# Causal attention and a channel mix on one core: the eight PSUM banks in one pool, batch 0 in two column ranges, and another order of the start

## The chip, the core and the metric

The kernel runs on one core of one Trainium2 chip. The metric is the device time of one execution in microseconds. The core has a matrix engine (TensorE, PE in the profile), which writes its products to PSUM, a memory of eight banks of 128 x 512 fp32; VectorE (DVE), ScalarE (ACT) and GpSimd (POOL), which work on tiles of 128 partitions in SBUF (DVE and ACT read PSUM too); SyncE (SP), which here only issues transfers; and 16 DMA engines, which serve the transfers issued from SP, ACT and POOL. Every engine runs its own list of instructions in order and waits for the others by semaphores.

## What is computed

Block-causal attention of eight batches, and over its output a channel mix (RWKV style):

```python
# q, k, v: (8 batches, 8 heads, 576, 64); blocks of 64 positions
scores = q @ k.T / sqrt(64)            # only where block(row) >= block(column)
attn   = softmax(scores) @ v
x      = attn as (8, 576, 512)
x_prev = x shifted by one position
xk = mu_k * x + (1 - mu_k) * x_prev    # and xr with mu_r
k  = relu(xk @ w_k)                    # 512 -> 1024
out = sigmoid(xr @ w_r) * (k * k @ w_v)
```

## The kernel before

Each batch goes through these steps, and each step is a *task* that the code adds to a list (`plan.add`), with the engine that it runs on, the tiles that it uses and the tasks that it needs.

* `qkld`: four loads per batch, half of q's or k's heads each (0.59 MB in fp32). Batch 0's come from SP as two transfers each and are cast to bf16 by `qkc` (L229). Those of batches 1 to 7 are casting transfers issued from POOL (L274). `turn` (L292) transposes 32 x 32 blocks on DVE.
* `vld` (L314), `vc` (L229, L223): v in two halves, two transfers each from SP, and a cast to fp16.
* `sc` (L396): scores, in *units* of up to 512 columns of all heads. A unit takes two pairs of banks, half of the heads in each. For batches 0 and 1 the two halves are tasks of their own. `ex` (L417): two exponentials per unit on ACT, which write tile `e`.
* For batches 1 to 7, `av` (L480 for the sums, L491 for the products with v), then the sums' reciprocals (L436, L441, L450 on DVE) and `norm` (L520, L528). For batch 0, the 576 positions are done in three thirds: `sum` (L554), `av` (L568), `norm` (L582).
* The mix: `d` (the difference to the position before, L608, L604) and `mul` (L624, L628), by 128 channels.
* The channel mix by groups `c` of 512 rows: `pk` (L661: eight products with the K weights), `relu` (L674, L676), `sq` (L683, L685), `pr` and `tanh` (L700, L709), `pv` (L730: products with the V weights), `o` (L738) and `store`. Group 0's `pk` is done for 192, 192 and 128 rows.
* `wld`, `wc`: the weights K, R, V are loaded from SP (L252) as fp32 and cast on DVE, ACT or POOL. `mus` loads mu_k and mu_r from SP (L760), `mu1` makes four small tiles of them on DVE.

Nothing decides at run time. `ORDER` is a list of task numbers, in which the instructions are written; each engine gets its own in that order. `PLACE` gives the engine of each task that may go to several. Tiles are in rings (`RINGS`): a task that needs a tile gets, among those that no later-listed task still uses, the one that has been free longest. PSUM has three rings: `s` (two pairs of banks, for scores), `av` (one pair, for the attention products) and `mm` (two single banks, for everything else).

In `ORDER`, a number may have "+n": n products of an identity matrix that nobody reads, ahead of the task (`unread`, L235). In the kernel before no number has it.

At the start, the order on the engines is: SP: batch 0's `qkld`, the first `vld`, two K weights, `mus`, the second `vld`, the other K weights, then v of batches 2 and 1 among the V weights, the R weights last. POOL: four `qkld` of batch 1 and one of batch 2, then a `qkc` of batch 0, more loads, casts. PE: scores of batch 0 with some of batch 1 among them, sums, batch 0's products with v, the rest of batch 1's scores, `pk 0 6`.

Of the kernel before, what the change touches and what calls it, by code (L numbers as in the profile page):

```python
# [66 lines left out]
    "DDPDAPDPAPAPAADAPDPPADPPPPDPPPPDAAAPAAPDPPADDPDPDPPPADADDPPPDAAPDDAPAD"  # L67
    "AADPDAAPADAADADPDDDPAPDAAADAAPDAAAAPAPDPAPDPAAAADPAAAPDDDAAPDPDPAPAPAP"
    "DPAAAADAAPAAAPDDAADDDAAPAAADAPAPDPDAAPDPAADPAAAAAPAPDPAPADAPADAAAAAPDA"
    "DAAAADADDDADAAAPAPAPAPADAAAAADDDAPDP")  # L70


class Plan:
# [17 lines left out]
    def buf(self, ring):  # L91
        return {"ring": ring, "left": 0, "slot": None}

    def issue(self, t):


        for b in t["uses"]:
            if b["slot"] is None:
                ring = self.slots[b["ring"]]
                at = min((s[0], n) for n, s in enumerate(ring) if s[1])[1]  # L100
                ring[at][1] = False
                b["slot"] = at
        t["fn"](t["eng"], t)
        self.issued += 1
        for b in t["uses"]:
            b["left"] -= 1
            if not b["left"]:
                self.slots[b["ring"]][b["slot"]] = [1000 + self.issued, True]
# [18 lines left out]
def kernel(  # L127
# [31 lines left out]
    RINGS = {"ld": 6, "nb": 5, "qkt": 2, "vo": 2, "e": 9, "xt": 1, "tt": 1,  # L159
             "rc": 2, "rt": 1, "d": 2, "xk": 2, "xr": 2, "kr": 4, "k2": 2,  # L160
             "t": 4, "o": 3, "s": 2, "av": 1, "mm": 2}
    plan = Plan(RINGS)
    pools = {}
    for n in RINGS:
        if n in ("xk", "xr"):
            continue
        kw = {"space": PSUM} if n in ("s", "av", "mm") else {}
        pools[n] = ctx.enter_context(
            tc.tile_pool(name="p_" + n, bufs=1, **kw))
# [5 lines left out]
        "ld": ([P, LW], FP), "nb": ([P, LW], BF),  # L175
# [5 lines left out]
        "s": ([P, 2, 512], FP), "av": ([P, 2, 512], FP), "mm": ([P, CH], FP)}  # L181
# [3 lines left out]
             for at in range(n)}  # L185

    def new(buf):

        return slots[buf["ring"], buf["slot"]]
# [43 lines left out]
    spare = {}  # L233

    def unread(t, dst):  # L235

        for _ in range(t["fill"]):
            nc.tensor.matmul(  # L240
                spare.get("at", dst), identb,
                identb[:, :].unsqueeze(1).to_broadcast([P, 4, P]),
                start=True, stop=True)

    def load(key, jobs, nbytes):
        ld = plan.buf("ld")

        def fn(eng, me):  # L250
            for dst, src in jobs(new(ld)):
                nc.sync.dma_start(dst, src)  # L252
        return ld, add(key, ("SP",), fn, uses=[ld], kind="ld",
                       kb=nbytes / 1024, starts=1 if key[4] in "kr" else 2)
# [7 lines left out]
    def add_qk(b, g, n):  # L262
# [4 lines left out]
        ld, nb = plan.buf("ld"), plan.buf("nb")  # L267
# [4 lines left out]
        if b in DIRECT:  # L272
# [3 lines left out]
                    uses=[nb], kind="ldc", kb=P * LW * 4 / 1024)  # L276
        else:
            def fetch(eng, me):
                if b not in HALVES:
                    nc.sync.dma_start(new(ld), rows(GH * g, GH))  # L280
                    return
                for y in range(2):
                    nc.sync.dma_start(new(ld)[y * D:y * D + D],  # L283
                                      rows(GH * y + 2 * g, 2))
            t = add(f"qkld {b} {g} {n}", ("SP",), fetch, uses=[ld], kind="ld",
# [18 lines left out]
    def add_v(b, m):  # L304
# [3 lines left out]
        ld = plan.buf("ld")  # L308
# [24 lines left out]
    def add_w(name, i):  # L333
        if name == "k":
            srcs = [by_quarter(moe_w_k)[i // 2, i % 2]]
        elif name == "r":
            srcs = [moe_w_r.rearrange("(g p f) j -> g p (f j)", g=2, f=2)[i]]
        else:
            srcs = [moe_w_v[(2 * i + h) * P:(2 * i + h + 1) * P]
                    for h in range(2)]  # L340
        w = 2 * CH // len(srcs)
        ld, t = load(f"wld {name} {i}", lambda d: [
            (d[:, h * w:h * w + w], s) for h, s in enumerate(srcs)],
            P * 2 * CH * 4)

        def fn(eng, me):
            s = new(ld)[:, 0:2 * CH]
            if name == "k":
                convert(eng, WK[:, i], s)
            else:  # L350
                dst = (WR if name == "r" else WV)[:, 2 * i:2 * i + 2]
                convert(eng, dst, s.rearrange("p (h j) -> p h j", h=2),
                        0.5 if name == "v" else None)
# [480 lines left out]
```

## Time and profile before

| | |
|---|---|
| median of three runs | 286.56 us (286.09 to 289.16) |
| profiled execution | 286.35 us, of which 284.6 us from the first to the last instruction |
| PE busy | 247.6 us (87%), 4232 matmuls |
| DVE, ACT, POOL busy | 197.6, 175.3, 84.1 us (69%, 62%, 30%) |
| mean granted clock of PE | 0.934 |
| HBM read, written | 33.56 MB, 9.44 MB |

In the profile's rows an instruction has its engine, the line of the kernel, what it writes <- what it reads and the shapes. "x48" is the number of instructions that a row holds. Timeline rows begin with the start and the time from the first to the last of them; what ended the idle time before stands in square brackets, and "issue" means that nothing in the profile shows a wait. Group rows give the busy time and the mean of one in ns. Rows of the chain that ended last begin with start and length, and name engine, tile and line. SPq is SP's queue.

### The profile page before, as it was taken

Reading aid. Unit: us, or ns where it says so; the run is one execution under the profiler, and the core shown is the slowest. Engines: PE = TensorE matmul, PEld = TensorE weight load, DVE = VectorE, ACT = ScalarE, POOL = GpSimd, SP = SyncE. Lnnn points to the kernel's source line nnn. Section 1 sums busy time; section 2 is a strip of 40 time slices with the busy share of each in tenths; the row PEclk is TensorE's granted clock in tenths of the full one; section 3 lists DMA queues with packets and bytes.
Section 4 is the critical chain, followed back from the end, with each engine's and each line's share of the span. In section 5 each row is a group of like instructions: output and inputs, shape, how many; then the busy total and the mean of one; then the engine's idle time right before and its main releaser. Section 6 shows DMA issues by size and latency. Waiting matters only on the chain.

```text
span 284.6 us, 9493 instructions
## 1 busy us (share of the span) xinstructions
PE 247.6 (87%) x4232; PEld 136.8 (48%) x4232; DVE 197.6 (69%) x288; ACT 175.3 (62%) x252; POOL 84.1 (30%) x105
## 2 busy tenths in 40 slices
PE   0056865795889999999999999999999999999995
PEld 0055633563654545465454545754445575444452
DVE  1674344678688899795899788988657779744332
ACT  1059552578598297887557877867775847465410
POOL 4032040235480347173333231411152022024100
PEclk9998575577799999999999999999999999999999
DMA  7999999576999998898238012003001200300123
GB/s 180 246 238 245 244 198 206 134 139 148 234 195 212 234 202 143 172 194 165 78 86 151 7 74 76 2 5 113 37 2 39 87 31 1 113 37 1 74 94 129
DMA packets 49977, 35.35 MB, mean 124 GB/s; under 512 B 39312, under 2 KB 39568, under 8 KB 49936
## 3 DMA queue, kind: packets, MB, share of 16 engines
q1 hardware_dynamic: 45904, 26.49, 38.7%
q0 software_dynamic: 4032, 8.26, 17.1%
q8 instruction: 33, 0.54, 0.8%
q14 instruction: 8, 0.07, 0.1%
HBM read 33.56 MB, written 9.44 MB: 151 GB/s over the span
## 4 chain that ended last, share of the span: by engine, by line
PE 79%; SPq 7%; DMA 5%; issue 4%; ACT 3%; DVE 1%; POOL 0%; DVEq 0%; ACTq 0%; POOLq 0%
PE t_mm L661 24%; PE t_mm L730 21%; PE t_mm L700 12%; PE t_s L396 9%; PE t_av L491 7%; DMA t_ld<-in_v_dram 5%; PE t_av L480 4%; SPq L314 3%; PE t_av L568 2%; SPq L283 2%; ACT t_e L417 2%; SPq L252 2%; DVE t_kr L676 1%; ACT t_kr L674 1%; POOL t_vo L229 0%
## 5 line engine op out<-in xcount | busy, mean ns | idle before, releaser
L417 ACT ACTIVATE t_e<-t_s 128x1024 f16<-128x1024 f32 (+3 forms) x96 | 89.3, 968 | 45.8 <-PE t_s L396 45.1
L661 PE MATMUL t_mm<-t_xk,WK 128*128 128x512 f16 (+4 forms) x448 | 72.9, 313 | 1.9 <-DVE t_kr L676 1.3
L396 PE MATMUL t_s<-t_qkt 32*64 32x192 bf16 (+7 forms) x1424 | 43.9, 308 | 26.2 <-DVE t_qkt L292 16.4
L730 PE MATMUL t_mm<-WV,t_k 128*128 128x512 f16 (+1 forms) x296 | 66.4, 374 | 0.0
L685 POOL TENSOR_TENSOR t_k<-t_kr 128x512 f16<-128x512 f32 (+2 forms) x41 | 37.0, 913 | 84.8 <-ACT t_kr L674 50.8
L661 PEld LDWEIGHTS <-WK 128*128 128x128 f16 x448 | 39.9, 101 | 30.6 <-issue 8.4
L396 PEld LDWEIGHTS <-t_qkt 32*64 32x64 bf16 x1424 | 25.6, 115 | 43.8 <-issue 23.7
L730 PEld LDWEIGHTS <-t_k 128*128 128x128 f16 x296 | 28.0, 98 | 32.2 <-issue 0.6
L674 ACT ACTIVATE t_kr<-t_mm 128x512 f32<-128x512 f32 (+2 forms) x57 | 30.1, 531 | 20.1 <-PE t_mm L661 18.5
L709 ACT ACTIVATE t_t<-t_mm 128x512 f32<-128x512 f32 x36 | 21.5, 597 | 29.8 <-PE t_mm L700 29.0
L292 DVE STREAM_TRANSPOSE t_qkt<-t_nb 128x576 f32<-128x576 f32 x32 | 38.2, 1243 | 1.9 <-POOL t_nb L229 1.8
L738 DVE SCALAR_TENSOR_TENSOR t_o<-t_t,t_mm 128x512 f32<-128x512 f32 (+1 forms) x37 | 24.7, 670 | 19.0 <-PE t_mm L730 18.1
L700 PE MATMUL t_mm<-WR,t_xr 128*128 128x512 f16 x144 | 36.4, 380 | 0.4 <-ACT t_t L709 0.3
L608 POOL TENSOR_TENSOR t_d<-t_xt 128x576 f32<-128x576 f32 (+1 forms) x17 | 16.9, 999 | 52.8 <-DVE t_xk L628 19.4
L676 DVE TENSOR_SCALAR t_kr<-t_mm 128x512 f32<-128x512 f32 (+2 forms) x31 | 17.4, 564 | 16.2 <-PE t_mm L661 16.0
L528 DVE TENSOR_TENSOR t_xt<-t_av,t_rt 128x1024 f32<-128x1024 f32 x14 | 17.1, 1221 | 8.1 <-PE t_av L491 8.1
L491 PE MATMUL t_av<-t_e,t_vo 64*32 64x512 f16 (+7 forms) x1120 | 21.8, 284 | 0.2 <-issue 0.2
L628 DVE SCALAR_TENSOR_TENSOR t_xr<-t_d,MUR,t_xt 128x576 f16<-128x576 f32 (+1 forms) x29 | 20.8, 722 | 0.6 <-POOL t_d L608 0.6
L700 PEld LDWEIGHTS <-t_xr 128*128 128x128 f16 x144 | 12.8, 97 | 15.3 <-issue 1.6
L628 DVE SCALAR_TENSOR_TENSOR t_xk<-t_d,MUK,t_xt 128x576 f16<-128x576 f32 (+1 forms) x29 | 19.9, 690 | 0.2
L491 PEld LDWEIGHTS <-t_vo 64*32 64x32 f16 x1120 | 14.4, 92 | 10.9 <-issue 5.7
L683 ACT ACTIVATE t_k<-t_kr 128x512 f16<-128x512 f32 (+2 forms) x32 | 16.5, 530 | 1.3 <-DVE t_kr L676 0.7
(46 smaller groups left out, 165.9 us busy)
## 6 DMA issues: line engine op xcount, KB each, us to landing
t_ld<-in_v_dram SPq DMA_DIRECT2D x32, 288.0 KB, 6.4
out_dram<-t_o SPq DMA_DIRECT2D x35, 256.0 KB, 2.0
t_nb<-in_q_dram POOLq DMA_DIRECT2D x14, 288.0 KB, 6.7
t_nb<-in_k_dram POOLq DMA_DIRECT2D x14, 288.0 KB, 7.3
t_ld<-in_moe_w_k_dram SPq DMA_DIRECT2D x4, 512.0 KB, 7.9
t_ld<-in_moe_w_v_dram SPq DMA_DIRECT2D x8, 256.0 KB, 4.5
t_ld<-in_q_dram SPq DMA_DIRECT2D x4, 288.0 KB, 8.2
t_ld<-in_k_dram SPq DMA_DIRECT2D x4, 288.0 KB, 8.5
```

The source lines that it names most:

```text
L292: nc.vector.transpose(new(qkt)[:, n, g].rearrange("p t e -> p (t e)").bitcast(FP).rearrange("p (r j) -> p j r", r=RW), new(nb)[:, :].bitca ...
L396: nc.tensor.matmul(new(ms[a // 2])[y * D:y * D + D, a % 2, col:col + n], qkt[rows, 1, g, t * D:t * D + D, f], qkt[rows, 0, g, q0:q0 + n, f ...
L417: nc.scalar.activation(new(e)[:, 2 * h:2 * h + 2, 0:w], new(ms[h])[:, :, 0:w], AF.Exp, scale=ISQ)
L491: nc.tensor.matmul(PA[o, u, HALF + f * D:HALF + f * D + D] if kind == "T" else PA[o, u, lo - D:lo - D + n], weight(b, u, c, t % JT, f), E[ ...
L628: e.scalar_tensor_tensor(dst, dt[:, 0, 0:W], (MUK1, MUR1)[n][:, cc:cc + 1], x, ALU.mult, ALU.add)
L661: nc.tensor.matmul(ps[:, a:a + n], WK[:, cc, jc * P:(jc + 1) * P], MIX[0][:, cc, at:at + n], start=(cc == 0), stop=(cc == CCn - 1))
L674: nc.scalar.activation(kt, ps, AF.Relu)
L685: (nc.vector if eng == "DVE" else nc.gpsimd).tensor_tensor(dst, KR, KR, ALU.mult)
L700: nc.tensor.matmul(ps, MIX[1][:, cc, g % XW:g % XW + P], WR[:, cc], start=(cc == 0), stop=(cc == CCn - 1))
L709: nc.scalar.activation(new(tb), new(m), AF.Tanh, scale=0.5)
L730: nc.tensor.matmul(ps[:, 0:w], k2[:, jc, jt * P:(jt + 1) * P], WV[:, jc, cols], start=(jc == 0), stop=(jc == JCn - 1))
L738: nc.vector.scalar_tensor_tensor(new(o)[:, 0:w], new(tiles["tbf", c, jt])[:, cols], 1.0, new(m)[:, 0:w], ALU.add, ALU.mult)
```

## The change

1. **PSUM.** The three rings become one, `ps`, with eight banks. Scores and attention products take a pair (`size` 2), all other products a single bank, preferably one whose neighbour is in use.
2. **Batch 0 in two parts**: positions 0 to 191 and 192 to 575, instead of thirds. The second part's scores are five units of pieces up to 384 wide; its products with v are two tasks, one for each half of the channels (`f`). The mix of batch 0 is in the same two ranges, and group 0's `pk` is done for 192 and 320 rows.
3. **Weights.** K and R are casting transfers issued from POOL, straight into their fp16 tiles, with no cast task. V stays on SP with a cast, with one transfer for two blocks instead of two. Of batch 0's loads one is issued from ACT.
4. **Rings of SBUF tiles.** The six fp32 load tiles are split into four for q, k and weights (`lq`) and two for v (`lv`); the tiles of cast q and k (`nb`) are four instead of five.
5. **Unread products.** 72 in all: 36 at the very start, 9 ahead of batch 0's second sums, 17 in ones and twos among the scores of batches 0 and 1 and ahead of one product of batch 0, and 10 from the first `pk` on (2, 6, 1, 1).
6. **Order and places** are new.

```diff
+    def take(self, b):
+        ring = self.slots[b["ring"]]
+        if b["size"] == 2:
+            at = min((max(ring[2 * p][0], ring[2 * p + 1][0]), p)
+                     for p in range(len(ring) // 2)
+                     if ring[2 * p][1] and ring[2 * p + 1][1])[1]
+        elif b["size"] == 1:
+            at = min((ring[n ^ 1][1], s[0], n)
+                     for n, s in enumerate(ring) if s[1])[2]
...
-    RINGS = {"ld": 6, "nb": 5, "qkt": 2, "vo": 2, "e": 9, "xt": 1, "tt": 1,
+    RINGS = {"lq": 4, "lv": 2, "nb": 4, "qkt": 2, "vo": 2, "e": 9, "xt": 1, "tt": 1,
...
-             "t": 4, "o": 3, "s": 2, "av": 1, "mm": 2}
+             "t": 4, "o": 3, "ps": 8}
...
+        "ps": ([P, 2, CH], FP)}
...
+                e = nc.sync if eng == "SP" else nc.scalar
...
+                    e.dma_start(new(ld)[y * D:y * D + D],
+                                rows(GH * y + 2 * g, 2))
...
-            srcs = [by_quarter(moe_w_k)[i // 2, i % 2]]
+            dst, src = WK[:, i], by_quarter(moe_w_k)[i // 2, i % 2]
...
         cast["w", name, i] = add(
-            f"wc {name} {i}", ("DVE", "ACT") if name == "v" else ALL, fn, [t],
-            uses=[ld], kind="cast", cols=2 * CH)
+            f"wld {name} {i}", ("POOL",),
+            lambda eng, me: nc.gpsimd.dma_start(dst, src), kind="ldc",
+            kb=P * 2 * CH * 4 / 1024, starts=1)
...
+    PARTS = [(0, 192), (192, 576)]
+    PIECES = [
+        [[(0, 0, 0, 192), (192, 1, 64, 128), (320, 2, 128, 64)]],
+        [[(0, 0, 192, 384), (384, 7, 448, 128)],
+         [(0, 1, 192, 384), (384, 8, 512, 64)],
+         [(0, 2, 192, 384), (384, 5, 320, 128)],
+         [(0, 3, 192, 384), (384, 5, 448, 128)],
+         [(0, 4, 256, 320), (320, 6, 384, 192)]],
+    ]
...
-        ms = [plan.buf("s") for _ in range(2)]
+        ms = [plan.buf("ps", 2) for _ in range(2)]
...
+        groups = [(0, 1)] if 2 * W <= 512 else [(0,), (1,)]
+        for fs in groups:
+            am = plan.buf("ps", 2)
...
-    SUBS = {0: [(0, 192), (192, 384), (384, 512)]}
+    SUBS = {0: [(0, 192), (192, 512)]}
...
-        m, kr = plan.buf("mm"), plan.buf("kr")
+        m, kr = plan.buf("ps", 1), plan.buf("kr")
```

The start in the new order, engine by engine (task, batch, then its part; "+n" are the unread products):

```
SP:   qkld 0 (k, then q of the first heads, then q of the others), vld 0, vld 0, mus,
      vld 1, vld 1, V weights x4, vld 2, ...
ACT:  qkld 0 (k of the other heads), ex 0 part 0, ex 0 part 1 ..., d 0, d 0, ex 1 x11, relu, ex 1, tanh, ...
POOL: qkc 0, qkc 0, qkld 1 x4, d 0, K weights x4, R weights x2, d 0, qkld 2 x4, ...
DVE:  qkc 0, turn 0, turn 0, qkc 0, turn 0, turn 0, vc 0, reciprocals of part 0, vc 0, mu1, norm 0 part 0,
      turn 1, mul, turn 1, turn 1, mul, turn 1, reciprocals of part 1, mul x3, norms of part 1, mul, d, ...
PE:   +36, sc 0 x6, +1 sc 0, +2 sc 0, sum 0 part 0, +2 sc 0, sc 0 x2, +1 av 0 part 0, +1 sc 0, +9 sum 0 part 1,
      av 0 part 1 x2, sc 1 x12 (with +10 among them), +2 pk 0, pr 0, pk 0 x4, av 1 S, pk 0 x3, av 1 T, A, B, ...
```

More of the change, by code (lines that the diff above doesn't have):

```diff
@@ L98, in issue @@
             if b["slot"] is None:
[L99 to L102, printed above, removed]
+                self.take(b)
         t["fn"](t["eng"], t)
@@ L107, in issue @@
             if not b["left"]:
-                self.slots[b["ring"]][b["slot"]] = [1000 + self.issued, True]
+                self.mark(b, 1000 + self.issued)
     def order(self):
@@ L184 @@
              for ring, n in RINGS.items() if ring in SHAPES
-             for at in range(n)}
+             for at in range(n // 2 if ring == "ps" else n)}
     def new(buf):
-        return slots[buf["ring"], buf["slot"]]
+        at = buf["slot"]
+        if buf["size"] == 1:
+            return slots[buf["ring"], at // 2][:, at % 2]
+        return slots[buf["ring"], at]
     identb = consts.tile([P, P], BF)
@@ L240, in unread @@
             nc.tensor.matmul(
-                spare.get("at", dst), identb,
+                dst, identb,
                 identb[:, :].unsqueeze(1).to_broadcast([P, 4, P]),
                 start=True, stop=True)
[L247 to L254, printed above, removed]
     qkt_buf = [plan.buf("qkt") for _ in range(B)]
@@ new lines, in add_w, with convert @@
+        cast["w", name, i] = add(
+            f"wld {name} {i}", ("POOL",),
+            lambda eng, me: nc.gpsimd.dma_start(dst, src), kind="ldc",
+            kb=P * 2 * CH * 4 / 1024, starts=1)
+    WHOLE = [
[6 rows of a table added]
+    ]
+    PARTS = [(0, 192), (192, 576)]
+    PIECES = [
[6 rows of a table added]
+    ]
+    SPLIT = (0, 1)
+    HALVES = (0,)
+    DIRECT = range(1, B)
+    add = plan.add
+    tiles, cast, ready, evac = {}, {}, {}, {}
+    ALL = ("POOL", "DVE", "ACT")
+    def convert(eng, dst, src, scale=None):
+        if eng == "ACT":
+            if scale is None:
+                nc.scalar.copy(dst, src)
+            else:
+                nc.scalar.activation(dst, src, AF.Copy, scale=scale)
+            return
+        e = nc.vector if eng == "DVE" else nc.gpsimd
+        if scale is None:
+            e.tensor_copy(dst, src)
+        else:
+            e.tensor_scalar_mul(dst, src, scale)
@@ new lines, in unread, with add_qk, rows, fetch @@
+    def unread(t, dst):
+        for _ in range(t["fill"]):
+            nc.tensor.matmul(
+                dst, identb,
+                identb[:, :].unsqueeze(1).to_broadcast([P, 4, P]),
+                start=True, stop=True)
+    qkt_buf = [plan.buf("qkt") for _ in range(B)]
+    vo_buf = [plan.buf("vo") for _ in range(B)]
+    xt_buf = [plan.buf("xt") for _ in range(B)]
+    def add_qk(b, g, n):
+        src, qkt = (q, k)[n], qkt_buf[b]
+        ld, nb = plan.buf("lq"), plan.buf("nb")
+        def rows(h0, count):
+            return src[b, h0:h0 + count].rearrange(
+                "y (r j) d -> (y r) (j d)", j=TOK)
+        if b in DIRECT:
+            t = add(f"qkld {b} {g} {n}", ("POOL",),
+                    lambda eng, me: nc.gpsimd.dma_start(
+                        new(nb), rows(GH * g, GH)),
+                    uses=[nb], kind="ldc", kb=P * LW * 4 / 1024, starts=1)
+        else:
+            def fetch(eng, me):
+                e = nc.sync if eng == "SP" else nc.scalar
+                if b not in HALVES:
+                    e.dma_start(new(ld), rows(GH * g, GH))
+                    return
+                for y in range(2):
+                    e.dma_start(new(ld)[y * D:y * D + D],
+                                rows(GH * y + 2 * g, 2))
+            t = add(f"qkld {b} {g} {n}", ("SP", "ACT"), fetch, uses=[ld],
+                    kind="ld",
+                    kb=P * LW * 4 / 1024, starts=2 if b in HALVES else 1)
+            t = add(f"qkc {b} {g} {n}", ALL,
+                    lambda eng, me: convert(eng, new(nb), new(ld)), [t],
+                    uses=[ld, nb], kind="cast", cols=LW)
+        def turn(eng, me):
+            nc.vector.transpose(
+                new(qkt)[:, n, g].rearrange("p t e -> p (t e)").bitcast(
+                    FP).rearrange("p (r j) -> p j r", r=RW),
+                new(nb)[:, :].bitcast(FP).rearrange(
+                    "p (j s) -> p j s", s=RW))
+        evac["qkt", b, g, n] = add(f"turn {b} {g} {n}", ("DVE",), turn, [t],
+                                   uses=[nb, qkt], kind="turn", cols=S)
@@ new lines, in place, with add_v, fetch @@
+    def place(b, a, y):
+        return (a // 2, a % 2 + 2 * y) if b in HALVES else (y, a)
+    def add_v(b, m):
+        ld = plan.buf("lv")
+        c0 = 2 * m
+        w = 2 * JT * D
+        def fetch(eng, me):
+            for u in range(2):
+                nc.sync.dma_start(
+                    new(ld)[u * D:u * D + D, 0:w].rearrange(
+                        "p (c t d) -> p c t d", c=2, d=D),
+                    v[b, 4 * u:4 * u + GH].rearrange(
+                        "c (t p) d -> p c t d", p=D)[:, c0:c0 + 2])
+        t = add(f"vld {b} {m}", ("SP",), fetch, uses=[ld], kind="ld",
+                kb=P * w * 4 / 1024, starts=2)
+        def fn(eng, me):
+            convert(eng, new(vo_buf[b])[:, c0:c0 + 2],
+                    new(ld)[:, 0:w].rearrange("p (c t d) -> p c t d", c=2,
+                                              d=D))
+        cast["v", b, m] = add(f"vc {b} {m}", ALL, fn, [t],
+                              uses=[ld, vo_buf[b]], kind="cast", cols=w)
@@ new lines, in by_quarter, with add_w, halves @@
+    def by_quarter(w):
+        return w.rearrange("(g p f) j -> g f p j", g=2, f=2)
+    def add_w(name, i):
+        if name == "k":
+            dst, src = WK[:, i], by_quarter(moe_w_k)[i // 2, i % 2]
+        elif name == "r":
+            dst = WR[:, 2 * i:2 * i + 2].rearrange("p f j -> p (f j)")
+            src = moe_w_r.rearrange("(g p f) j -> g p (f j)", g=2, f=2)[i]
+        else:
+            ld = plan.buf("lq")
+            def halves(x):
+                return x.rearrange("p (h j) -> p h j", h=2)
+            t = add(f"wld v {i}", ("SP",), lambda eng, me: nc.sync.dma_start(
+                halves(new(ld)[:, 0:2 * CH]),
+                moe_w_v[2 * i * P:(2 * i + 2) * P].rearrange(
+                    "(h p) j -> p h j", p=P)), uses=[ld], kind="ld",
+                kb=P * 2 * CH * 4 / 1024, starts=1)
+            cast["w", name, i] = add(
+                f"wc v {i}", ("DVE", "ACT"), lambda eng, me: convert(
+                    eng, WV[:, 2 * i:2 * i + 2],
+                    halves(new(ld)[:, 0:2 * CH]), 0.5), [t], uses=[ld],
+                kind="cast", cols=2 * CH)
+            return
@@ L354, in add_w @@
         cast["w", name, i] = add(
[L355 to L356 removed]
+            f"wld {name} {i}", ("POOL",),
+            lambda eng, me: nc.gpsimd.dma_start(dst, src), kind="ldc",
+            kb=P * 2 * CH * 4 / 1024, starts=1)
     WHOLE = [
@@ L559, in add_third @@
                 kind="avS", cols=[sum(j[2] for j in jobs)])
-        def fn(eng, me):
-            PA = new(am)
-            unread(me, PA[:, 0])
-            for f in range(2):
-                for t, q0, n, col, e in jobs:
-                    for c in range(GH):
-                        for u in range(2):
-                            nc.tensor.matmul(
-                                PA[c * QC:(c + 1) * QC, u, f * THIRD + q0 - lo:
-                                   f * THIRD + q0 - lo + n],
-                                weight(b, u, c, t, f),
-                                new(e)[u * D:u * D + D, c, col:col + n],
-                                start=t == 0, stop=t == last)
```

151 lines of the change are left out of this document (85 added, 66 removed), and 100 rows, old and new, of tables (ORDER, WHOLE).

## Prediction

> **What bounds the kernel now.** I read first the page's forty slices, 7.1 us each, then the table of stretches.
>
> ```profile
> span 284.6 us, 9493 instructions
> PE   0056865795889999999999999999999999999995
> PEclk9998575577799999999999999999999999999999
> DMA  7999999576999998898238012003001200300123
> ```
>
> ```profile
> core 0: us, PE busy (x) PEld busy (x) DVE busy (x) ACT busy (x) POOL busy (x), PEclk, DMA share, GB/s
> 40.00:56.00 16.00, 10.98 (x366) 7.86 (x366) 8.55 (x16) 6.24 (x7) 2.70 (x5) 0.52 0.98 188
> 56.00:62.00 6.00, 6.00 (x97) 4.20 (x95) 3.74 (x8) 4.91 (x10) 1.13 (x2) 0.57 0.48 96
> 62.00:70.00 8.00, 5.12 (x72) 3.13 (x71) 6.56 (x17) 6.17 (x10) 4.18 (x7) 0.87 0.96 182
> 70.00:78.00 8.00, 6.74 (x154) 4.86 (x152) 5.32 (x11) 4.62 (x13) 4.01 (x6) 0.70 0.82 208
> 78.00:100.00 22.00, 21.19 (x320) 10.99 (x319) 19.02 (x28) 15.26 (x26) 9.50 (x16) 1.00 1.13 213
> 140.00:180.00 40.00, 40.00 (x670) 20.40 (x672) 35.69 (x46) 29.17 (x40) 11.28 (x11) 1.00 0.32 84
> ```
>
> From about 100 us PE is full at full clock: its products set the rest of the time, and other engines can only make it wait. Before 56 us DMA is full and PE is not. Between 56 and 100 us PE is nearly full but loses 2.88, 1.26 and 0.81 us to idling (stretch less busy time) and some 5.3 us to a lower clock (6.00 x 0.43 + 5.12 x 0.13 + 6.74 x 0.30). So a change of the start shortens the run by as much as it brings forward the first channel-mix product (L661) with the same work done before it. I call that moment T0. The orders of instructions of both kernels have batches 0 and 1's scores and batch 0's value products ahead of T0, so T0 compares like with like. The timeline of the start:
>
> ```profile
> 16.39 1.92 PE L396 MATMUL t_s<-t_qkt 32*64 32x192 bf16 x48 [16.39 <-DVE t_qkt L292]
> ...
> 40.26 0.66 PE L396 MATMUL t_s<-t_qkt 32*64 32x512 bf16 x5 [2.48 <-issue]
> 40.85 2.27 PE L568 MATMUL t_av<-t_e,t_vo 64*32 64x192 f16 x123
> 45.91 0.73 PE L568 MATMUL t_av<-t_e,t_vo 64*32 64x64 f16 x37 [2.79 <-issue]
> ...
> 55.96 1.46 PE L661 MATMUL t_mm<-t_xk,WK 128*128 128x192 f16 x8
> ```
>
> ```profile
> 1.42 0.72 POOL L274 DMA_DIRECT2D t_nb<-in_q_dram  x1
> ...
> 18.03 1.14 POOL L229 CAST t_nb<-t_ld 128x1152 bf16<-128x1152 f32 x1 [8.55 <-DMA t_ld<-in_q_dram]
> ...
> 35.43 1.15 POOL L229 CAST t_vo<-t_ld 128x1152 f16<-128x1152 f32 x1 [10.63 <-DMA t_ld<-in_v_dram]
> ```
>
> T0 is 55.96 us. Batch 0's q and k share DMA with batch 1's from 1.42 us on, so the last of its four tiles is cast at 18.03 us. Its second half of v, queued behind weights, is cast at 35.43 us, and all of batch 0's products with v wait for that. The idle PE marked "issue" before 40.26 and 45.91 us waits for no engine: between those starts it ran 5 + 123 = 128 matmuls.
>
> ```profile
> q8 instruction: 33, 0.54, 0.8%
> ```
>
> 33 packets for PE's 4232 matmuls is one per 128. I read these gaps as PE waiting for its own instructions behind full DMA queues, about 2.6 us a time.
>
> **Part by part: the start.** Removed ahead of T0: batch 1's loads beside batch 0's. POOL now first casts two tiles of batch 0 and only then issues them. One tile of batch 0 is issued from ACT. DMA rates come from these two windows (6 to 14 us, then 20 to 30 us); a casting load (q0) counts its written half, so it reads twice that.
>
> ```profile
> q1 hardware_dynamic: 347, 1.30, 60.5%
> q0 software_dynamic: 347, 0.72, 47.1%
> ```
>
> ```profile
> q0 software_dynamic: 550, 1.15, 61.8%
> q1 hardware_dynamic: 1725, 1.27, 49.2%
> ```
>
> Over 8 us 1.30 + 1.44 MB were read, 342 GB/s; the plain queue by its share alone, 1.30/0.605/8 us, gives 268 GB/s. I take 290. Batch 0's q and k are 2.36 MB (4 x 0.59), first bytes at about 2 us: last tile at 10.4 us, the two that the first scores need at about 8.4 (one ACT tile is interleaved). Then a POOL cast and a turn:
>
> ```profile
> L292 DVE STREAM_TRANSPOSE t_qkt<-t_nb 128x576 f32<-128x576 f32 x32 | 38.2, 1243 | 1.9 <-POOL t_nb L229 1.8
> ...
> L417 ACT ACTIVATE t_e<-t_s 128x1024 f16<-128x1024 f32 x78 | 76.9, 1021 | 43.9 <-PE t_s L396 43.3
> L417 ACT ACTIVATE t_e<-t_s 128x640 f16<-128x640 f32 x14 | 9.3, 701 | 1.8 <-PE t_s L396 1.8
> L417 ACT ACTIVATE t_e<-t_s 128x896 f16<-128x896 f32 x2 | 1.8, 914 | 0.1
> L417 ACT ACTIVATE t_e<-t_s 128x768 f16<-128x768 f32 x2 | 1.6, 815 | 0.0
> ```
>
> 8.4 + 1.14 + 1.24 = 10.8 us for the first score (16.39 before), 11.5 for the first exponential. Up to four score tiles are in flight now instead of two, so ACT runs through batch 0's twelve: 8 x 1.02 + 2 x 0.91 + 2 x 0.82 = 11.6 us, to 23.1.
>
> Two waits could break that run. The product of part 0 with v stands on PE ahead of the last score, with everything else of PE behind it. v (1.18 MB) follows q and k on SP directly: 3 us alone at 188 GB/s (the stretch 40 to 56 us), then beside batch 1's loads at 127 (second window), so at 18 us; it is needed at 20.5. Later than that, everything slips one for one. The mu loads now stand behind v on SP, and on DVE mu's four small operations block norm, batch 1's turns and, through the part's differences, POOL's weight issues:
>
> ```profile
> 20.16 0.47 SPq L760 DMA_DIRECT2D MUR<-in_moe_mu_r_dram  x1
> ...
> 31.15 0.17 DVE L766 TENSOR_SCALAR MUR<-MUR 128x4 f32<-128x4 f32 x1 [2.41 <-DMA MUR<-in_moe_mu_r_dram]
> ```
>
> They took 11 us there, behind weights and v; behind v's tail I take 21 us for their arrival (up to 25).
>
> ```profile
> L582 DVE TENSOR_TENSOR t_xt<-t_av,t_rt 128x768 f32<-128x768 f32 x3 | 2.9, 958 | 7.7 <-PE t_av L568 7.7
> L628 DVE SCALAR_TENSOR_TENSOR t_xk<-t_d,MUK,t_xt 128x192 f16<-128x192 f32 x11 | 4.9, 445 | 0.0
> ...
> L274 POOL DMA_DIRECT2D t_nb<-in_q_dram x14 | 8.0, 573 | 20.5 <-DVE t_qkt L292 20.4
> ```
>
> Norm (0.96), four turns (4 x 1.24) and two mix operations (2 x 0.45) end at 27.9 us; batch 1's q and k (2.36 MB, issued from 12 us) are there by 24.
>
> PE after the exponentials of batch 0:
>
> ```profile
> 33.57 1.47 PE L554 MATMUL t_mm<-t_e,pick 128*32 128x192 f16 x40
> ```
>
> Part 1's sums are 40 matmuls, wider than these: 1.5 to 3 us, I take 1.6. Its products with v are 160 matmuls at 18.5 ns (2.27/123), 3.0 us, up to twice that for twice the width; I take 4. The nine unread products ahead of the sums run while ACT finishes. This stretch holds two 128-matmul boundaries: 0 to 5.6 us, I take 4, the weights' traffic being on. So 23.1 + 1.6 + 4 + 4 + 0.8 (two unread products, first score) = 33.5 for batch 1's first exponential, after its turns. Batch 1's twelfth score needs a pair of banks that the eighth exponential frees: 33.5 + 8 x 1.02 = 41.7. T0 is 42 us, 14 earlier.
>
> Moved and hidden: six weight loads (K, R; 3.1 MB), from SP with casts on three engines, to casting loads from POOL. Six issues of 0.57 us stand behind batch 0's first difference on POOL (22.5 us); the K weights (2.1 MB) land 9.1 us later at the 230 GB/s that the second window read, plus 1.5 to start: 33 to 35 us. They have 7 us of cover by batch 1's exponentials; without it T0 moves one for one. Removed: six casts of weights on three engines, none on the path. The V weights go out in four transfers instead of eight, needed long after T0. One slot fewer for batch loads ("nb") costs nothing: later batches load 40 us ahead.
>
> **The rest.** Batch 0's channel mix in two column ranges instead of three: 32 of 96 matmuls go, the columns stay.
>
> ```profile
> 78.71 0.65 PE L661 MATMUL t_mm<-t_xk,WK 128*128 128x128 f16 x8 [0.22 <-DVE t_kr L676]
> ...
> 244.22 3.45 PE t_mm L730 x16
> ```
>
> At 81 ns each 2.6 us at most, 0 at least (if only columns count); I take 1.6. Ten unread products after T0 at 0.216 us (3.45/16) cost 2.2, or nothing where PE would wait. Together +0.6.
>
> Between 56 and 100 us 10.2 us were lost. DVE was busy 3.74 + 6.56 + 5.32 + 19.02 = 34.6 us of them. Summing the groups' durations in program order from T0 to the last V product of the first 512 rows, I get 35 us of DVE beside 30.5 of PE before, and 25 beside 26 in the new order: casts and part of batch 0's mix are gone or ahead of T0, so DVE no longer leads. I take 4 us of the loss back; bounds 10 back (none lost) and -5 (ACT's and DVE's queues meet the denser scores).
>
> What the clock does there weighs little. The stretch 56 to 62 us kept PE full for 6 us at a granted 0.57. The Trainium skill, "TensorE: Matmul & The Clock Gate", Part 1, says that some 3.4 us of sustained work release the half rate: by it the new start would lose 1.7 us to the clock, by the row 2.6, and the sum would be 1 us less by the rule. The trace doesn't bear the shorter time out.
>
> **Sum** against the profiled execution, 286.35 us with a span of 284.6 (the median of the runs is 286.56): 286.35 - 14.0 + 0.6 - 4.0 = 269.0.
>
> **Shared banks** I cost at nothing. Every product of PE now takes any free bank, scores two pairs per unit. In the new order 15 of the 36 units of batches 2 to 7 ask for a pair that the first exponential of the unit before must free, one V product (8 x 0.216 = 1.73 us) after it; that takes 1.02. The cover is the 0.7 us between; an exponential that stands later in ACT's queue takes it away.
>
> **Rivals.**
> (a) The late load: v or mu takes the place of the wait removed. v at 22 and mu at 25 us, the products at 6 us, the boundaries at 5.6: T0 = 42 + 2 + 2 + 2 to 3 = 49, time 276. For it: v took 13 us last time. Against: it queued behind a megabyte of weights.
> (b) A clean dense stage: all 10 us back and T0 at 41: 262. For it: the 40 us from 140 on are without a gap. Against: DVE at 25 of 26 us.
> (c) It doesn't do what it says: the transfers are hidden anyway. Ahead of T0 10.2 MB must land (batches 0 and 1, K, R); at 188 GB/s that is 54 us, the weights last: T0 = 54, and with nothing taken back later the time is 285. Against: the K weights need only 8 MB landed, and 342 GB/s were read at the start.
> (d) Slower: the shared banks. ACT falls behind by tanh, relu and casts put ahead of exponentials; PE, in order, stops at each of the 15 close units with all products behind it. From a mean stop of 1.35 us per unit (20 us) the gain is gone; at 1.5 us: 291. For it: by the same sums ACT's work is 88% of PE's in the new order from there through batch 4's rows. Against: two pairs for scores alone left no gap from 140 us on, with ACT at 29.17 of 40.
>
> **How the numbers follow.** The forecast (264 to 275) 0.54, (a) 275 to 283 0.18, (b) 258 to 264 0.12, (c) 283.7 to 289.4 0.05, (d) 0.11. The range 259 to 283 leaves out (c), (d) and a little of (b). Runs differ by about 1%, so that is what can be told from no change: faster 0.84, same 0.05, slower 0.11.
>
> **What would show it.** Right: first score at 10 to 12 us, v's second cast by 20, the first channel-mix product at 39 to 46 with K weights landed before 38, PE above 95% from 60 us on. Wrong: PE waiting for ACT's exponentials in every batch (d); DVE held at mu past 25 us or the part's v product past 22 (a); the first channel-mix product waiting for a weight load (c).

## The result and the profile after

| | before | after |
|---|---|---|
| median of four runs each | 287.44 us (286.09 to 289.16) | 301.49 us (299.6 to 304.21) |
| profiled execution, its span | 286.35 us, 284.6 us | 299.6 us, 297.8 us |
| first channel-mix product (T0) | 55.96 us | 51.00 us |
| mean granted clock | 0.934 | 0.966 |

The ratio after to before is 1.0463, with a 95% interval from 1.0362 to 1.0564: slower, where 269.0 us had been forecast. Some executions of a kernel are slower than the others (of after, 304.21 us): they count in the medians but not in the ratios, and the profiles of e2 and e4 below are of such executions. The page of the kernel after: its span, the forty slices (7.4 us each) and PE's instruction packets.

```profile
span 297.8 us, 9076 instructions
PE   8689489999998998998999889898988999886763
PEclk9979855999999999999999999999999999999999
q8 instruction: 31, 0.51, 0.7%
```

Before, PE's row was nothing but nines from 100 us on, up to its last slice. Now eights stand among them all the way and it falls to 6 and 7 near the end, while the clock is full. The table of stretches of the kernel after, columns as in the prediction:

```profile
36.00:51.00 15.00, 13.90 (x172) 5.39 (x171) 5.77 (x12) 10.19 (x11) 2.68 (x3) 0.50 1.08 264
51.00:56.00 5.00, 5.00 (x91) 3.99 (x90) 2.24 (x6) 2.32 (x6) 0.00 (x0) 0.89 0.73 116
56.00:100.00 44.00, 41.23 (x718) 20.91 (x716) 37.12 (x45) 33.86 (x53) 24.20 (x30) 1.00 0.81 145
100.00:297.80 197.80, 172.33 (x2561) 88.74 (x2559) 125.98 (x170) 116.30 (x169) 35.75 (x36) 1.00 0.34 80
```

The same of the kernel before:

```profile
56.00:100.00 44.00, 39.05 (x637) 23.18 (x635) 34.65 (x63) 30.95 (x56) 18.83 (x29) 0.86 0.95 190
100.00:284.60 184.60, 180.82 (x2756) 93.00 (x2754) 135.76 (x178) 119.99 (x172) 52.30 (x52) 1.00 0.33 81
```

This splits the 13.2 us by which the span grew. T0 came 5.0 us earlier. From T0 on PE is busy for 218.56 us (5.00 + 41.23 + 172.33) instead of 219.87, 1.3 less. But its idle time there (stretch less busy) is 0 + 2.77 + 25.47 = 28.2 us instead of 4.95 + 3.78 = 8.7, so 19.5 more: -5.0 - 1.3 + 19.5 = 13.2. Nearly all of it lies after 100 us, where the kernel before lost 3.78 us in all, the tail included.

What ended those waits of PE, from 100 us on (total us, times, longest; the first four of after, and all that the same view names for before):

```profile
PE t_ps L834 <- ACT t_kr L847: 4.5, 6, 0.9
PE t_ps L873 <- DVE t_o L911: 4.3, 6, 1.0
PE t_ps L903 <- DVE t_o L911: 3.8, 6, 0.8
PE t_ps L903 <- ACT t_t L882: 3.4, 5, 0.7
```

```profile
PE t_av L491 <- issue: 0.2, 1, 0.2
```

PE waits for relu (L847), tanh (L882) and `o` (L911): the readers of single banks. No exponential is in that view, nor in its seven rows that are left out here. The timeline shows why a reader so short can stop PE. This is a piece of the last 33 us of the kernel after:

```profile
265.44 1.02 PE L834 MATMUL t_ps<-t_xk,WK 128*128 128x512 f16 x4 [0.69 <-ACT t_kr L847]
266.56 0.60 ACT L847 ACTIVATE t_kr<-t_ps 128x512 f32<-128x512 f32 x1 [1.17 <-PE t_ps L834]
267.20 1.89 PE L903 MATMUL t_ps<-WV,t_k 128*128 128x512 f16 x8 [0.74 <-ACT t_kr L847]
269.13 0.69 DVE L849 TENSOR_SCALAR t_kr<-t_ps 128x512 f32<-128x512 f32 x1 [2.76 <-PE t_ps L903]
269.87 1.89 PE L903 MATMUL t_ps<-WV,t_k 128*128 128x512 f16 x8 [0.78 <-DVE t_kr L849]
...
281.29 1.89 PE L903 MATMUL t_ps<-WV,t_k 128*128 128x512 f16 x8 [0.78 <-DVE t_o L911]
283.21 0.69 DVE L911 SCALAR_TENSOR_TENSOR t_o<-t_t,t_ps 128x512 f32<-128x512 f32 x1 [1.98 <-PE t_ps L903]
283.96 1.89 PE L903 MATMUL t_ps<-WV,t_k 128*128 128x512 f16 x8 [0.78 <-DVE t_o L911]
```

The order here is `pk 8 6` in bank 1, `pk 8 7` in bank 0, relu of 8 6, `pv 7 0` in bank 1, relu of 8 7, `pv 7 1` in bank 0. The relu on DVE at 269.13 reads the K product that was done at 266.46 (265.44 + 1.02). It starts only when the V product in the *other* bank ends, at 267.20 + 1.89 = 269.09. The V product after it, at 269.87, waits in turn for this relu. So product and reader alternate although two banks are in use: from 281.29 a V product comes every 2.67 us instead of the 1.73 (8 x 0.216) of the kernel before. The two banks are the halves of one tile since the change (`new` returns `[:, at % 2]`), and `take` looks for a bank whose neighbour is in use, which leads single products into one pair.

The theory from this (A): two banks that are one tile wait for each other, a product in one half for the reader of the other and the other way round. Rival (B): the shared pool or the order gives the stops, the halves do not matter.

### The profile page after: what moved, and what is told of

It is laid out like the page before. It is cut to its first block, busy times and chain, and to the rows that moved or that the text cites. A ratio compares the mean times of both kernels' runs of the same rounds, so it can differ in the third digit from the quotient of the medians.

```text
span 297.8 us, 9076 instructions
## 1 busy us (share of the span) xinstructions
PE 258.8 (87%) x4056; PEld 133.5 (45%) x4056; DVE 190.6 (64%) x266; ACT 176.2 (59%) x255; POOL 74.5 (25%) x91
## 3 DMA queue, kind: packets, MB, share of 16 engines
q1 hardware_dynamic: 44816, 22.75, 32.5%
## 4 chain that ended last, share of the span: by engine, by line
PE 73%; DVE 10%; ACT 7%; issue 5%; DMA 3%; SPq 1%; POOL 0%; DVEq 0%; ACTq 0%; POOLq 0%
PE t_ps L834 21%; PE t_ps L903 20%; PE t_ps L873 10%; PE t_ps L563 9%; PE t_ps L658 6%; PE t_ps L413 4%; DVE t_o L911 4%; PE t_ps L647 3%; DMA t_lq<-in_q_dram 3%; ACT t_t L882 3%; ACT t_kr L847 2%; DVE t_qkt L458 2%; DVE t_kr L849 1%; ACT t_e L584 1%; DVE t_xt L695 1%
## 5 line engine op out<-in xcount | busy, mean ns | idle before, releaser
L584 ACT ACTIVATE t_e<-t_ps 128x1024 f16<-128x1024 f32 (+3 forms) x96 | 87.8, 973 | 33.4 <-PE t_ps L563 33.3
L834 PE MATMUL t_ps<-t_xk,WK 128*128 128x512 f16 (+5 forms) x416 | 69.0, 315 | 8.8 <-ACT t_kr L847 5.6
L903 PE MATMUL t_ps<-WV,t_k 128*128 128x512 f16 (+1 forms) x296 | 67.6, 373 | 9.0 <-DVE t_o L911 3.9
L834 PEld LDWEIGHTS <-WK 128*128 128x128 f16 x416 | 37.0, 98 | 36.2 <-issue 12.4
L847 ACT ACTIVATE t_kr<-t_ps 128x512 f32<-128x512 f32 (+2 forms) x61 | 31.8, 553 | 29.7 <-PE t_ps L834 17.1
L911 DVE SCALAR_TENSOR_TENSOR t_o<-t_t,t_ps 128x512 f32<-128x512 f32 (+1 forms) x37 | 24.2, 669 | 35.8 <-PE t_ps L903 26.0
L903 PEld LDWEIGHTS <-t_k 128*128 128x128 f16 x296 | 27.9, 97 | 42.8 <-issue 13.2
L882 ACT ACTIVATE t_t<-t_ps 128x512 f32<-128x512 f32 x36 | 20.8, 598 | 39.6 <-PE t_ps L873 22.9
L563 PE MATMUL t_ps<-t_qkt 32*64 32x64 bf16 (+7 forms) x1328 | 40.0, 310 | 3.6 <-DVE t_qkt L458 2.9
L873 PE MATMUL t_ps<-WR,t_xr 128*128 128x512 f16 x144 | 36.1, 381 | 5.0 <-DVE t_o L911 4.3
L849 DVE TENSOR_SCALAR t_kr<-t_ps 128x512 f32<-128x512 f32 (+2 forms) x19 | 12.0, 643 | 30.7 <-PE t_ps L834 17.9
L413 PE MATMUL t_ps<-identb 128*128 128x512 bf16 x72 | 22.6, 442 | 3.4 <-ACT t_e L584 1.9
L802 DVE SCALAR_TENSOR_TENSOR t_xk<-t_d,MUK,t_xt 128x576 f16<-128x576 f32 (+2 forms) x26 | 21.4, 830 | 1.1 <-POOL t_d L782 1.0
L658 PE MATMUL t_ps<-t_e,t_vo 64*32 64x64 f16 (+7 forms) x1120 | 21.3, 284 | 0.8 <-issue 0.6
## 6 DMA issues: line engine op xcount, KB each, us to landing
WK<-in_moe_w_k_dram POOLq DMA_DIRECT2D x4, 256.0 KB, 10.3
```

The source lines that it names most:

```text
L413: nc.tensor.matmul(dst, identb, identb[:, :].unsqueeze(1).to_broadcast([P, 4, P]), start=True, stop=True)
L563: nc.tensor.matmul(new(ms[a // 2])[y * D:y * D + D, a % 2, col:col + n], qkt[rows, 1, g, t * D:t * D + D, f], qkt[rows, 0, g, q0:q0 + n, f ...
L584: nc.scalar.activation(new(e)[:, 2 * h:2 * h + 2, 0:w], new(ms[h])[:, :, 0:w], AF.Exp, scale=ISQ)
L658: nc.tensor.matmul(PA[o, u, HALF + f * D:HALF + f * D + D] if kind == "T" else PA[o, u, lo - D:lo - D + n], weight(b, u, c, t % JT, f), E[ ...
L802: e.scalar_tensor_tensor(dst, dt[:, 0, 0:W], (MUK1, MUR1)[n][:, cc:cc + 1], x, ALU.mult, ALU.add)
L834: nc.tensor.matmul(ps[:, a:a + n], WK[:, cc, jc * P:(jc + 1) * P], MIX[0][:, cc, at:at + n], start=(cc == 0), stop=(cc == CCn - 1))
```

## The experiments

Ratios are to the kernel before, run again on the same chip: 13 runs (median 287.01 us) for the first four, 16 (285.2 us) for the last two. Added lines shift the line numbers: by 2 in e1, by 4 in e2, e4 and e5, by 8 in e6.

**e1: the kernel before, with its two single banks as halves of one tile.** Nothing else is changed: same order, same rings.

```diff
-        ... "mm": ([P, CH], FP)}
+        ... "mm": ([P, 2, CH], FP)}
...
-             for at in range(n)}
+             for at in range(1 if ring == "mm" else n)}
...
+        if buf["ring"] == "mm":
+            return slots["mm", 0][:, buf["slot"]]
```

> The kernel before, with one thing changed: the two single banks for products (ring mm) are the two halves of one tile instead of two tiles. Same banks, same order, same work. Theory A (two banks that are one tile wait for each other: a reader of one half waits for the product in the other half that stands earlier in the program, and the next product waits for that reader): each of some 150 mix products that has no scores or attention products behind it to cover costs about 0.7 us more; with half of them covered 286 + 75 x 0.7 = 340 us (310 to 380), and PE waits for relu, tanh and o after 100 us, where it waited 0.2 us. Rival B (the loss of the changed kernel comes from its order and from picking few banks, the tile has no part in it): 286 us within 1%, no new waits.

Measured: 364.05 us (362.87 to 365.24), ratio 1.2726 (1.2571 to 1.2881). PE's waits after 100 us, and a piece of its timeline:

```profile
PE t_mm L663 <- ACT t_kr L676: 16.1, 24, 1.0
PE t_mm L702 <- DVE t_o L740: 11.9, 13, 2.1
```

```profile
303.40 1.02 PE L663 MATMUL t_mm<-t_xk,WK 128*128 128x512 f16 x4 [0.69 <-ACT t_kr L676]
...
304.51 0.60 ACT L711 ACTIVATE t_t<-t_mm 128x512 f32<-128x512 f32 x1 [1.16 <-PE t_mm L663]
305.16 1.02 PE L663 MATMUL t_mm<-t_xk,WK 128*128 128x512 f16 x4 [0.73 <-ACT t_t L711]
```

The same alternation appears, in a kernel that has no shared pool and the old order: the tanh at 304.51 waits for a K product that it does not read (released at 304.42 by the product from 303.40), and the K product at 305.16 waits for that tanh. PE's idle time after 100 us is 263.40 - 197.93 = 65.5 us, from 3.78. Theory A is shown. Few banks alone are not the cause: the kernel before has the same two single banks, as tiles of their own, in the same order, and idles for 3.78 us. That the price is larger than in the kernel after fits that here all single products have only these two halves, and there four pairs.

```profile
100.00:363.40 263.40, 197.93 (x2840) 98.75 (x2832) 143.39 (x189) 121.05 (x174) 54.73 (x55) 0.99 0.24 59
```

The Trainium skill, "PSUM — Partial Sum Buffer", section "PSUM bank collisions raise a hardware error", asks for semaphores by bank and quadrant, "by bank is the simple version". By that rule two halves of a tile, each a bank, would need no wait for each other. The waits here go by tile, and the measurement decides.

**e2: the kernel after, another choice of the single bank.** Tiles stay pairs, order and everything else stay; only which bank a single product gets is changed: one in the pair whose last taking is longest ago.

```diff
-            at = min((ring[n ^ 1][1], s[0], n)
+            at = min((self.touch[n // 2], s[0], n)
                      for n, s in enumerate(ring) if s[1])[2]
...
+        if b["size"]:
+            self.taken += 1
+            self.touch[at if b["size"] == 2 else at // 2] = self.taken
```

> The changed kernel with one rule of its bank choice changed: a single bank is taken in the pair whose last product is longest ago, instead of beside a bank in use. Order, engines and work are the same. Theory A: neighbours in time no longer share a pair, so most of the 24 us of waits of PE after the first channel-mix product go: about 282 us (276 to 288), first channel-mix product still at about 51 us. Rival B' (the evacuating engines are late because of the new order itself): the waits stay, 298 to 302 us.

Measured: 284.1 us (281.14 to 286.61), ratio 0.9897 (0.9791 to 1.0002). By the medians that is 17.4 us less than the kernel after (301.49). T0 in its timeline, the stretch from 100 us on, and the largest wait left in it:

```profile
50.18 0.84 PE L838 MATMUL t_ps<-t_xk,WK 128*128 128x192 f16 x4
```

```profile
100.00:284.80 184.80, 173.76 (x2584) 89.81 (x2568) 127.75 (x171) 119.26 (x171) 36.37 (x36) 0.99 0.37 86
```

```profile
PE t_ps L838 <- DVE t_o L915: 2.0, 1, 2.0
```

Idle time there falls from 25.47 to 11.04 us (10.32 in e5 below, which keeps the rule). The rule for single banks is thus what made the kernel slower than before; with it changed, the rest of the change is worth about 1%, at the edge of what the runs tell.

**e3: the kernel after without its 72 unread products.** The edit is `t["fill"] = 0` in `order`.

> The changed kernel without its 72 unread products. Theory F (in the stretch of batch 1's scores PE, at half clock, is the bound, and the 14 unread products there lie on the path): the first channel-mix product comes at about 47 us instead of 51, and the time falls by 4 to 6 us, to 295 us. Rival G (they keep the clock up and so pay for themselves): the granted clock between 10 and 36 us falls, the scores and sums of batch 0 slow down, first channel-mix product at 51 us or later, 299 to 303 us.

Measured: 297.79 us (297.77 to 297.81), ratio 1.041 (1.0291 to 1.0528). The median is 3.7 us below that of after, but the interval overlaps that of after (1.0362 to 1.0564): a gain is not told from none. The profiled spans differ by 1.8 us.

```profile
36.09 1.08 PE L563 MATMUL t_ps<-t_qkt 32*64 32x512 bf16 x13 [4.49 <-issue]
38.21 5.68 PE L563 MATMUL t_ps<-t_qkt 32*64 32x512 bf16 x120 [1.04 <-ACT t_e L584]
...
44.98 0.80 PE L834 MATMUL t_ps<-t_xk,WK 128*128 128x192 f16 x4 [0.17 <-ACT t_e L584]
```

T0 is 44.98, 6.0 us earlier than after. The unread products (12 ahead of T0 in this stretch, not the 14 expected) lie on the path to T0, as theory F says; rival G is out, as the granted clock is 1.00 from 10 to 30 us without them. But most of what is won is lost again behind T0: PE's idle time from there on is 32.5 us instead of 28.2 (-6.0 - 0.1 of busy time + 4.3 = -1.8).

**e4: both, spread single banks and no unread product.**

> Both edits together: banks spread over the pairs, and no unread products. Theories A and F add up: 282 - 5 = 277 us (270 to 284), below the kernel before by 3%. If A holds and G instead of F: 282 to 285. If neither: 298 or more.

Measured: 286.45 us (281.4 to 288.07), ratio 0.992 (0.9853 to 0.9987). The miss: 277 was expected. T0 is 3.8 us ahead of e2's 50.18, and the time is no better. In the two profiles PE's idle time from T0 on is 2.1 us longer than in e2 (17.9 against 15.8) and its busy time 1.9 us. Its T0 and its table of stretches:

```profile
46.36 0.80 PE L838 MATMUL t_ps<-t_xk,WK 128*128 128x192 f16 x4 [0.17 <-ACT t_e L588]
```

```profile
56.00:62.00 6.00, 3.73 (x81) 2.01 (x67) 4.29 (x6) 3.00 (x5) 1.26 (x2) 0.85 0.27 46
62.00:70.00 8.00, 7.74 (x43) 4.42 (x42) 5.24 (x6) 5.77 (x13) 4.71 (x7) 0.90 0.29 41
70.00:78.00 8.00, 5.80 (x75) 1.87 (x73) 7.24 (x10) 5.09 (x6) 3.47 (x6) 0.79 1.05 161
```

In these 22 us PE idles 4.7 us. The granted clock is lower as well (0.85, 0.90, 0.79), but e3, which has no unread product either, had 1.00 in the same three stretches: that the missing products lower it is not shown. The next run drops only the last 12 unread products ahead of T0.

**e5: e2 without the last 12 unread products ahead of T0** (in `ORDER` the "+n" of tasks 109, 113, 115, 117, 127, 129, 131 and 474 goes; the other 60 stay).

> The kernel of e2 (a single bank is taken in the pair whose last product is longest ago) without the 12 unread products that stand among batch 1's scores and ahead of the first channel-mix product; the other 60 stay. Rows behind it: in e2 these 12 take about 6.2 us there (0.61 us alone and 1.01 to 1.03 for two, at a granted clock of 0.50), and T0 is 50.2; in e4, which has no unread product at all, T0 is 46.4, but from 52 to 78 us PE idles 4.7 us and loses 2.6 us to a lower clock (3.73 x 0.15 + 7.74 x 0.10 + 5.80 x 0.21), against 3.5 and 0.4 in e2. Theory F (the products among the scores lie on the path, and those after T0 hold the clock up): T0 at 45 to 47, granted clock 0.95 or more from 56 to 78 us, time about 280 (277 to 283). Rival G (a limit behind T0, DVE's chain or the loads of batch 2 and the V weights, sets when the dense part begins): T0 at 45 to 47 as well, but PE's idle time from T0 to 78 us grows by the 4 us that T0 gains, time 284 (282 to 287) as e2.

Measured: 281.63 us (279.97 to 284.57), ratio 0.9861 (0.9797 to 0.9924), 1.4% below the kernel before. Timeline and one stretch:

```profile
35.30 0.67 PE L746 MATMUL t_ps<-t_e,t_vo 64*32 64x320 f16 x41 [4.93 <-issue]
...
37.02 1.94 ACT L588 ACTIVATE t_e<-t_ps 128x1024 f16<-128x1024 f32 x2 [6.50 <-PE t_ps L567]
...
46.13 0.80 PE L838 MATMUL t_ps<-t_xk,WK 128*128 128x192 f16 x4 [0.17 <-ACT t_e L588]
...
57.81 1.39 PE L662 MATMUL t_ps<-t_e,t_vo 64*32 64x64 f16 x73 [2.31 <-issue]
```

```profile
56.00:78.00 22.00, 17.93 (x228) 8.92 (x235) 17.28 (x21) 15.31 (x23) 9.40 (x14) 1.00 0.63 100
```

T0 and the clock (1.00) are as theory F says, though e3 had this clock without any unread product. The time lies in F's range (277 to 283), just under G's (282 to 287). G is right in part: PE's idle time from T0 to 78 us grows from 3.5 us in e2 to 5.8, by 2.3 of the 4 us that T0 gains. PE idles 4.07 us in this stretch, 2.31 of it at one wait marked "issue". Against e2 (ratios 0.9861 and 0.9897) the gain of about 1 us is within both intervals; how much of the 4 us of T0 comes through stays open.

**e6: e5 with the K and R weights issued 6 us later** (tasks 19 to 24 stand behind task 53 in `ORDER`).

> The kernel of e5 with the six loads of the K and R weights issued from POOL after batch 0's last difference of the first column range (at 32.9 us in e2) instead of after its first (26.4 us): this takes back the weights' lead, by about 6 us. In e2 they were issued from 26.8 to 30.0 us and landed 8 to 14 us later. Theory H (the lead had cover): K lands at about 44 us, before T0, so T0 stays within 1 us of e5's and the time within 2 us of it; PE's wait of some 4 us for its own instructions (idle put down to issue at 29.9 to 33.7 us in e2) stays as it is, since the batch's values and the V weights still fill the DMA. Rival I (the lead is needed): the first channel-mix product waits for a weight load, T0 at 49 to 52, time 4 to 6 us over e5's. Rival J (the weights' traffic is what delays PE's instructions): the wait for instructions falls under 1.5 us and batch 1's scores start 2 to 3 us earlier.

Measured: 281.54 us (280.48 to 284.07), ratio 0.9896 (0.9855 to 0.9938), the same as e5.

```profile
31.56 0.58 PE L750 MATMUL t_ps<-t_e,t_vo 64*32 64x320 f16 x41 [2.10 <-issue]
32.07 0.67 PE L571 MATMUL t_ps<-t_qkt 32*64 32x512 bf16 x16
...
41.88 0.89 PE L842 MATMUL t_ps<-t_xk,WK 128*128 128x192 f16 x3 [0.17 <-ACT t_e L592]
44.28 0.34 PE L842 MATMUL t_ps<-t_xk,WK 128*128 128x192 f16 x1 [1.51 <-DMA WK<-in_moe_w_k_dram]
45.00 1.04 PE L881 MATMUL t_ps<-WR,t_xr 128*128 128x512 f16 x2 [0.38 <-DMA WR<-in_moe_w_r_dram]
...
57.13 1.40 PE L666 MATMUL t_ps<-t_e,t_vo 64*32 64x64 f16 x73 [1.10 <-issue]
```

None of the three theories holds alone. J is right in kind: without the weights' traffic the wait marked "issue" falls from 4.93 to 2.10 us (not under 1.5) and batch 1's scores start 3.8 us earlier (32.07 instead of 35.90). I is right in kind as well: the first products then wait for K and R, 1.51 and 0.38 us in these rows. The first K product stands at 41.88, and by 57.13, when the last products of batch 1 with v start, the lead over e5 (57.81) is 0.7 us. The early weight loads neither help nor harm the time: they trade one wait for another. (H's time came true, for another reason than H gave.)

## Why the prediction was wrong

In the profiled execution the miss is 30.6 us (299.6 - 269.0): T0 is 9.0 us later than forecast (51.0 instead of 42), and from T0 to the end 18.2 us were added where 3.4 were to go (+0.6 - 4.0), a miss of 21.6.

**The step that failed: "Shared banks I cost at nothing".** It asked only when a *pair for scores* comes free, and put the cover at 0.7 us between an exponential and a V product. It never asked what a *single* product waits for when its bank is half of a tile. In the kernel after, PE idles 19.5 us more than before from T0 on; e2, with another choice of the single bank, takes 12.4 of them back (28.2 to 15.8 us). The diff shows both of what was needed, the tile `[P, 2, CH]` and the preference for a bank beside one in use. e1 shows the halves' wait by itself, and e2 that the preference sets how often it is paid. Rival (d) had the right place, the right sign and, with 291, a price too low; its mechanism was wrong: after 100 us PE waits for relu, tanh and `o`, and for no exponential.

**T0, the term of 14 us, was 5.0.** The rows of the kernel after:

```profile
11.20 1.14 POOL L405 CAST t_nb<-t_lq 128x1152 bf16<-128x1152 f32 x1 [9.89 <-DMA t_lq<-in_q_dram]
...
13.69 4.31 PE L563 MATMUL t_ps<-t_qkt 32*64 32x192 bf16 x104 [2.94 <-DVE t_qkt L458]
...
14.28 3.45 ACT L584 ACTIVATE t_e<-t_ps 128x768 f16<-128x768 f32 x4 [11.04 <-PE t_ps L563]
...
18.84 0.81 ACT L584 ACTIVATE t_e<-t_ps 128x768 f16<-128x768 f32 x1 [1.11 <-PE t_ps L563]
...
21.55 0.72 DVE L405 CAST t_vo<-t_lv 128x1152 f16<-128x1152 f32 x1
...
22.20 4.58 ACT L584 ACTIVATE t_e<-t_ps 128x896 f16<-128x896 f32 x5 [0.31 <-PE t_ps L563]
...
24.34 0.17 DVE L935 TENSOR_SCALAR MUR<-MUR 128x4 f32<-128x4 f32 x1 [2.00 <-DMA MUR<-in_moe_mu_r_dram]
...
34.76 0.73 PE L742 MATMUL t_ps<-t_e,t_vo 64*32 64x320 f16 x41 [4.43 <-issue]
...
37.51 1.94 ACT L584 ACTIVATE t_e<-t_ps 128x1024 f16<-128x1024 f32 x2 [7.33 <-PE t_ps L563]
...
51.00 0.84 PE L834 MATMUL t_ps<-t_xk,WK 128*128 128x192 f16 x4
```

- First tiles: the q tile is cast at 11.20, not 8.4, so the first exponential starts at 14.28 instead of 11.5: 2.8 us. The rate of 290 GB/s was too high: from 2 to 11.2 us the DMA moved 231 GB/s. (By its own figures the forecast would have had 8.1 and 10.1 us instead of 8.4 and 10.4.)
- Batch 0's exponentials end at 26.78 (the last group, 22.20 + 4.58), after 12.5 us instead of 11.6: 0.9 us. ACT did not run through: its work was 10.8 us, and it waited 1.7 for scores (1.11, 0.30 and 0.31).
- From there to batch 1's first exponential: 10.7 us, forecast 10.4, near by luck. The stop of 4 us at two boundaries was 4.43 at one; the products with v took 2.9 us instead of 4; the two unread products and the first score, at half clock, took 2.1 instead of 0.8. The last transfer of v landed at about 20.4 (forecast 18, needed at 20.5) and its cast stood behind the reciprocals on DVE until 21.55; mu was ready at 24.34 (forecast 21). The part's product with v came at 23.47, past the 22 us that rival (a) gave as its sign, but neither load set the path: the exponentials from 22.20 on ran without a gap, and batch 1's last turn ended at 30.44, before PE's stop did.
- From that exponential to T0: 13.5 us instead of 8.2 to 8.5, 5.0 of the miss. The forecast let ACT set the pace at 1.02 us per exponential and did not price PE. In the stretch from 36 to 51 us PE is busy for 13.90 of 15 us at a granted clock of 0.50, and the last 12 unread products ahead of T0, of which the forecast had priced two (it counted two more as after T0), stand there, most of them between the scores. e5 drops them, and the same stretch takes 9.1 us (37.02 to 46.13).

2.8 + 0.9 + 0.3 + 5.0 = 9.0.

**The transition from 56 to 100 us** went better than forecast. PE idles 2.77 us there instead of 4.95, and the clock is 1.00 instead of 0.86: 2.2 us, and some 5.5 of clock (0.14 x 39) less the 0.55 lost from 51 to 56, about 7 us back where 4 were taken. But PE's busy time after T0 fell by 1.3 only, where the clock alone gave back 4.9: 3.6 us of other work stand against the +0.6 forecast. What these are was not parted; by lines, the unread products (L413) alone are busy for 2.9 us there. Rival (b), the clean dense stage, came near up to 100 us (7 of its 10 us) and failed behind it. Rival (c) is out: the row of T0 shows no wait for a K weight in the kernel after.

**With the single banks spread** and the path to T0 freed (e5, profiled at 283.22), 14.2 us of the miss remain: 4.1 of T0, and 10.1 behind it. PE's idle time from 46 us on is 6.4 + 10.3 = 16.7 us against 8.7 in the kernel before. Some of it is still pairs that share a tile: in the 2.0 us behind `o` (L915, in e5 as in e2) `pk 7 1`, in bank 7, waits for the `o` that reads bank 6. Some is the wait marked "issue" (2.31); which part an own tile for each single bank would take away was not tried.

## What to carry to other kernels

When a change merges buffers into a larger tile, ask of every user of a part what it now waits for: an order kept tile by tile makes two banks one, and an allocator that packs small users beside each other then makes product and reader take turns. A gap that is "free" for filling work is free only at the clock and on the engine of that moment; price the filler in the stretch where it stands. And a gain at the start counts only as far as the next stage can begin earlier: check what that stage waits for besides.

## What the runs showed of the hardware

In the kernel after, the granted clock fell to 0.50 after PE had idled for 4.43 us, and stayed there from 36 to 51 us while PE was busy for 13.90 of 15.00 us; it came back with the channel mix (0.89 from 51 to 56). The kernel before had 0.52 from 40 to 56 us. The Trainium skill, "TensorE: Matmul & The Clock Gate", Part 1, says that an idle window of some 3.4 us halves the rate and some 3.4 us of sustained work restore it. This fall agrees with the first, but shorter idling had the same effect elsewhere: 0.51 from 27 to 28 us in the kernel before, with no gap over 1.02 us since PE's first product, and 0.53 from 243.7 to 246.0 us in e5 behind the gap of 2.00 us. With the second the trace does not agree: the work lasted four times as long. Why scores and unread products did not raise the clock is open.

The long stops marked "issue" come at fixed counts of matmuls, whatever products stand there. The one of 4.43 us in the kernel after follows the 479th matmul record; so do those of 2.48 us in the kernel before, 3.81 in e2, 4.49 in e3, 4.22 in e4, 4.93 in e5 and 2.10 in e6. Others follow the 607th (2.79 us, before) and the 863rd (2.31 us, e5): the counts differ by multiples of 128, as one instruction packet per 128 matmuls would have it. That supports the reading that PE waits for its own instructions there. After 100 us, at a DMA share of 0.33, no such stop of the kernel before is over 0.2 us; from 30 to 36 us the share is 1.04 in the kernel after. In e6 six weight loads (3.1 MB) had been moved out of that time, and the stop is 2.10 us instead of the 4.93 of e5.
